# Top-32 attention and a token/channel mixer on one core: 63 of 144 score tiles masked by an accumulating DMA

## The chip, the core and the metric

The kernel runs on one NeuronCore of a Trainium2 chip. Five engines work side by side, each through its own queue in order: TensorE (PE in the profile; PEld is its weight loads), VectorE (DVE), ScalarE (ACT), GpSimd (POOL) and SyncE (SP), which issues most of the DMAs. A DMA is issued by an engine's queue and carried out by 16 DMA engines that all queues share. The metric is the device time of one execution in microseconds (us); lower is better.

## What is computed

Eight batches, eight heads, 576 positions, head dimension 64. Attention keeps, for each query, the 32 largest of its 576 scores, takes a softmax over these and multiplies by v. The result is then sent through a mixer: a token MLP (576 to 256 to 576) and a channel MLP (512 to 1536 to 512), each with a residual.

```python
scores = scale * np.matmul(q, k.transpose(0, 1, 3, 2))
kth = np.partition(scores, -top_k, axis=-1)[..., -top_k:-top_k + 1]
scores = np.where(scores >= kth, scores, -1000000000.0)
attn = np.exp(scores - np.max(scores, axis=-1, keepdims=True))
attn = attn / (np.sum(attn, axis=-1, keepdims=True) + 1e-09)
x = np.matmul(attn, v)                    # heads side by side: (8, 576, 512)
xt = x.transpose(0, 2, 1)
h = np.maximum(xt @ w_tok1, 0.0) @ w_tok2
u = x + h.transpose(0, 2, 1)
out = u + np.maximum(u @ w_ch1, 0.0) @ w_ch2
```

## The kernel before

**Tiling.** Two heads form a pair (32 pairs), two pairs a block `m` (16 blocks). A tile is 128 query rows by 576 keys; two tiles that are treated together are a *duo*. A block has nine duos: four of each pair ("whole" duos, both heads of a pair), and one "cross" duo that gathers the last 64 rows of both pairs. That makes 144 duos, numbered by `i0` (the first of the duo's two tiles, 0 to 286).

**One duo, step by step** (function `scores`, L551, with its inner functions):

- PE computes the scores of both tiles into a set of four of the eight PSUM banks (L567). ACT rescales them onto a fixed grid into an SX buffer (`level`, L377, called from L589).
- DVE finds an upper threshold: each row is cut into seven segments, and the eight largest of each (MAX8, L604) are narrowed down to one value (L608 to L611). A small DVE instruction makes a bias of it (L705, by the helper `small`).
- ACT counts by a sum of signs how many scores lie above (L620). Small DVE instructions turn the count into scales (`gs`, `ws`, `as`, L705).
- POOL rewrites SX as whole numbers (L627), with a few filler columns behind them (L630), so that the eighth largest of the row, taken by DVE (L636), is the exact 32nd largest score. A last small instruction gives `nt`.
- The scores below that threshold are then masked, in one of two ways.

**Second scores** (104 duos; `swap` in the code). POOL writes, for each score, a byte: the upper byte of a bf16 number in U, zero where the score is kept and large where it is dropped (L645). PE multiplies U by a scaled identity into a second set of four banks (L577) and adds the scores once more (L583). ACT takes the exponential from these banks into Pm (L650); dropped scores come out as zero.

**Product** (40 duos, those in `KEEP` and the cross duos). ACT takes the exponential early, from SX, into E (L616; two slots), which has to be over before POOL overwrites SX. When the threshold is known, two small DVE instructions make per-tile offsets (`no`, L658), POOL writes a mask M (L662) and multiplies E by M into Pm (L667), tile by tile.

Either way SP then issues a DMA transpose of Pm into PT (L689; three Pm slots, eight PT slots). When the five PT of a pair are there, PE multiplies them by v (`pv`, L741), DVE normalizes into Xb (L757, L760). After each batch the mixer runs on PE and ACT in between the attention of the next (`mlp_ops`, L782 on; its largest groups are L937 and L889). The last duo is transposed by PE instead (L680). At the end, DVE judges whether all counts were in range (`judge`, L1029); if not, a slow exact version runs.

**What sets the order.** Nothing runs in the order of the program text. Every piece of work is registered by `plan.add` with an engine, a duration, a due time (`DUE` and `SHIFT`, tables of numbers by kind and place), its dependencies, and the buffers it takes (`acq`) and uses. `Plan.run` (L159) then simulates all engines and fixes each engine's order. DMAs are charged in it as one serial resource, `dma` us each, with a fixed flight time of 1.8 us. In holes of PE that it foresees before `WARM` = 126 us, it puts matmuls whose result nobody reads (`heat`, L1066) into a free bank, up to 80% of a hole. On the chip each engine follows its list; semaphores keep the dependencies.

**Loads.** q, k and v of a pair come by SP, three DMAs each (two heads, then the last 64 rows; L456 and L460) into two slots each; rows of 256 bytes, since the two heads are interleaved in the buffer. POOL casts v to bf16 (L477). The weights come by POOL's queue (L419, L425) early on.

Of the kernel before, what the change touches and what calls it, by code (L numbers as in the profile page):

```python
# [8 lines left out]
P = 128  # L9
# [15 lines left out]
LIFT = -84.0  # L25
# [10 lines left out]
DUE = dict(  # L36
    lq=-96.4, tq=-673.586, ck=-47.467, nh=217.705, vc=515.373, mm=-50.319, cp=-480.623, seg=513.347, rnd=-123.788,
    sg=-32.194, g=116.987, a=-30.312, w=-504.645, x=329.997, dum=-145.081, mx=-217.177, nt=-374.167, u=-739.903,
    re=-0.409, ex=-84.108, ex1=13.923, tr=-224.789, pv=-236.633, nm=-337.898, mlp=74.169, seg1=-0.307, rnd1=66.104,
    x1=169.067, sg1=49.192, mx1=-339.219, pace=-3.054, mla=-74.384, first=-565.875, part=-685.418, rest=-246.62,  # L40
)
SHIFT = {
    "g": (61.807, -147.375, 140.963, -181.697, 156.616, 26.724, 34.323, 11.941, -35.848, 30.887, 208.306, 84.613,
        107.569, -69.432, 265.313, -150.613, 114.386),
    "a": (-50.78, -120.215, 178.073, -19.932, 30.505, -54.302, 87.047, 124.772, 17.806, 20.373, -113.98, -8.761,
        -68.577, 30.101, -39.535, -52.774, 33.246),
    "w": (-82.752, 281.07, 97.131, 43.49, -64.563, -8.332, 77.683, 231.168, 80.7, 197.151, -50.471, -73.802,
        -43.931, -114.631, -79.541, -162.458, -113.427),
    "mm": (-184.435, -38.353, 19.694, 1.745, 3.982, 15.187, 12.503, -8.69, -0.528, 5.73, -6.328, 3.267, 8.751,
        -3.938, -4.406, 14.144, 7.483),  # L50
    "cp": (52.361, 99.626, -16.31, -173.284, -11.598, -9.737, 69.201, -56.919, 10.911, 98.911, 199.248, 263.088,
        -140.484, 22.964, 302.777, 94.767, -67.389),
    "seg": (-63.015, 30.613, 31.915, 51.581, 44.051, 26.738, -3.325, -34.051, 24.02, 1.666, -35.92, -21.112, -6.004,
# [1205 lines left out]
```

## Time and profile before

| | us |
|---|---|
| median of 3 runs | 759.12 |
| lowest and highest | 757.1, 759.3 |
| the profiled execution | 761.78 |
| its span, first to last instruction | 759.7 |

The profile lists each engine's busy time, the time in 40 slices, a chain of work followed back from the last instruction, groups of instructions by line with count, total busy time and mean duration of one, and DMA issues with their time to landing. Instructions of one engine overlap at their ends, so that a mean duration is longer than what one more instruction costs. A row of waits reads: who waited, for whom, total us, how many times, longest.

Some rows not used below, to fill in the picture: ACT's sign counts (L620) take 222.8 us in 288 instructions, POOL's whole numbers (L627) 234.3 us in 288, DVE's MAX8 of segments (L604) 378.1 us in 2016, and its MAX8 over whole rows (L636) 219.2 us in 288.

### The profile page before, as it was taken

What the parts mean: (1) busy time and instruction counts of PE and PEld (TensorE: products, weight loads), DVE (VectorE), ACT (ScalarE), POOL (GpSimd) and SP (SyncE); (2) the same over time, 40 slices, a digit from 0 to 9 for tenths busy, and PEclk for the clock granted to TensorE, in tenths of its full rate; (3) what the DMA queues carried; (4) which work ended last, traced back from release to release, by engine and by line L of the source; (5) the groups of instructions that cost most, each with busy time, mean ns of one, the idle gap of its engine ahead of it and who ended that gap; (6) DMA issues with size and microseconds to landing.
All of it is one profiled execution on the core that took longest, in us unless ns stands there. A gap on an engine that the chain in (4) does not pass through costs nothing.

```text
span 759.7 us, 23211 instructions
## 1 busy us (share of the span) xinstructions
PE 707.6 (93%) x7545; PEld 389.2 (51%) x7619; DVE 701.0 (92%) x4384; ACT 671.7 (88%) x1134; POOL 632.2 (83%) x859
## 2 busy tenths in 40 slices
PE   9888989999879999799999999989999999999995
PEld 4445545445545545445556455554556455555552
DVE  6999999999999999999999989999999989999621
ACT  5898889998989999989999989999999989998450
POOL 4889999999999989989999797987689887999400
PEclk9999999999999999899999999999999999999999
DMA  6865887766757668666666487858374578635431
GB/s 136 160 112 90 128 137 131 139 117 148 151 92 146 105 131 138 126 89 143 131 122 121 85 144 135 162 117 151 69 130 96 102 143 134 116 58 100 99 70 60
DMA packets 311297, 90.50 MB, mean 119 GB/s; under 512 B 305792, under 2 KB 307712, under 8 KB 311168
## 3 DMA queue, kind: packets, MB, share of 16 engines
q1 hardware_dynamic: 307344, 84.97, 59.9%
q0 software_dynamic: 3024, 3.77, 3.6%
q8 instruction: 61, 1.00, 0.5%
q14 instruction: 68, 0.56, 0.2%
q10 hardware_dynamic: 800, 0.20, 0.1%
HBM read 35.85 MB, written 9.44 MB: 60 GB/s over the span
## 4 chain that ended last, share of the span: by engine, by line
DVE 64%; PE 23%; ACT 9%; issue 2%; POOL 1%; DMA 1%; SPq 0%; ACTq 0%; POOLq 0%
DVE cd L604 28%; DVE tlo L636 18%; PE bank L889 5%; PE bank L937 5%; DVE cd L609 4%; ACT sg L620 3%; PE bank L567 3%; PE bank L583 3%; DVE thi L611 3%; DVE m L608 2%; DVE Xb L760 2%; ACT SX L377 2%; ACT Pm L650 2%; PE bank L741 1%; PE bank L577 1%
## 5 line engine op out<-in xcount | busy, mean ns | idle before, releaser
L604 DVE MAX8 cd<-SX 128x8 f32<-128x82 f32 (+1 forms) x2016 | 378.1, 231 | 4.2 <-ACT SX L377 4.0
L627 POOL TENSOR_SCALAR SX<-SX,nh,gs 128x576 int32<-128x576 f32 x288 | 234.3, 825 | 6.4 <-DVE as L705 2.5
L620 ACT ACTIVATE sg<-SX,nh 128x576 bf16<-128x576 f32 x288 | 222.8, 775 | 9.5 <-DVE nh L705 7.9
L636 DVE MAX8 tlo<-SX 128x8 uint32<-128x584 uint32 x288 | 219.2, 761 | 4.7 <-POOL SX L627 3.0
L645 POOL TENSOR_SCALAR U<-SX,nt,ws 128x576 uint8<-128x576 int32 x208 | 169.8, 830 | 22.4 <-DVE nt L705 8.2
L567 PE MATMUL bank<-kT,qT 64*64 64x288 f32 x2304 | 173.4, 416 | 12.1 <-ACT SX L377 6.2
L377 ACT ACTIVATE SX<-bank 128x1152 f32<-128x1152 f32 (+1 forms) x147 | 161.6, 1109 | 13.9 <-PE bank L567 10.8
L650 ACT ACTIVATE Pm<-bank 128x1152 bf16<-128x1152 f32 x104 | 117.2, 1127 | 23.0 <-PE bank L583 22.1
L583 PE MATMUL bank<-kT,qT 64*128 64x288 f32 x832 | 131.1, 434 | 0.0
L567 PEld LDWEIGHTS bank<-kT,qT 64*64 64x64 f32 x2304 | 77.6, 132 | 84.0 <-ACT SX L377 15.8
L667 POOL TENSOR_TENSOR Pm<-E,M 128x576 bf16<-128x576 bf16 x80 | 102.2, 1278 | 6.4
L889 PE MATMUL bank<-wc2b,H 128*128 128x512 bf16 x357 | 88.3, 380 | 3.7 <-issue 1.9
L937 PE MATMUL bank<-UT,wc1b 128*128 128x512 bf16 x353 | 87.9, 380 | 3.0 <-ACT SX L377 0.7
L583 PEld LDWEIGHTS bank<-kT,qT 64*128 64x128 f32 x832 | 72.6, 188 | 34.5 <-issue 24.0
L662 POOL TENSOR_SCALAR M<-SX,no,ws 128x576 int8<-128x576 int32 x80 | 66.1, 826 | 13.9 <-DVE no L658 13.2
L937 PEld LDWEIGHTS <-wc1b 128*128 128x128 bf16 x380 | 34.0, 98 | 51.6 <-issue 17.7
L889 PEld LDWEIGHTS <-H 128*128 128x128 bf16 x384 | 33.9, 98 | 50.8 <-issue 17.2
L577 PE MATMUL bank<-U,identN 64*64 64x288 bf16 x832 | 48.8, 299 | 11.2 <-ACT SX L377 5.4
L741 PEld LDWEIGHTS <-PT 128*128 128x128 bf16 x1600 | 53.0, 99 | 11.5 <-issue 8.1
L620 ACT ACTIVATION_READ_ACCUMULATOR sg<-SX,nh 128x1 f32 x288 | 56.3, 195 | 0.0
L741 PE MATMUL bank<-vb,PT 128*128 128x65 bf16 x1600 | 55.8, 195 | 0.4 <-ACT SX L377 0.2
L611 DVE MAX8 thi<-cd 128x8 f32<-128x42 f32 x288 | 54.8, 190 | 0.5
(124 smaller groups left out, 871.2 us busy)
## 6 DMA issues: line engine op xcount, KB each, us to landing
vL<-in_v_dram SPq DMA_DIRECT2D x64, 128.0 KB, 3.2
kL<-in_k_dram SPq DMA_DIRECT2D x63, 128.0 KB, 2.9
qL<-in_q_dram SPq DMA_DIRECT2D x62, 128.0 KB, 2.9
out_dram<-ob SPq DMA_DIRECT2D x14, 512.0 KB, 3.4
PT<-Pm SPq DMA_TRANSPOSE x143, 3.6
wc1b<-in_moe_w_ch_dram POOLq DMA_DIRECT2D x4, 384.0 KB, 4.8
wc2b<-in_moe_w_ch_dram POOLq DMA_DIRECT2D x4, 384.0 KB, 5.3
kL<-in_k_dram SPq DMA_DIRECT2D x32, 32.0 KB, 2.8
```

Source lines behind the costliest of these rows:

```text
L377: nc.scalar.activation(out=dst, in_=src, func=AF.Copy, scale=GRID, bias=-LEVEL * GRID)
L567: nc.tensor.matmul(out=row(s1.t, h, lo, lo + HS, c, 64), lhsT=x["qT"].t[r, q0 : q0 + 64], rhs=x["kT"].t[r, lo : lo + HS], start=True, stop ...
L583: nc.tensor.matmul(out=row(s2.t, h, lo, lo + HS), lhsT=x["qT"].t[r, q0 : q0 + P], rhs=x["kT"].t[r, lo : lo + HS], start=False, stop=True)
L604: ss.append(plan.add("DVE", 0.146, due["seg"] + DUE["seg1"] * h, lambda a=a, h=h, cd=cd: nc.vector.max(cd.t[:, a, :], Sb.t[:, h, bounds[a] ...
L620: return [plan.add("ACT", 0.775, due["sg"] + DUE["sg1"] * h, lambda i=i0 + h, h=h: nc.scalar.activation(out=sg[:, h, :], in_=Sb.t[:, h, 0: ...
L627: xo.append(plan.add("POOL", 0.828, due["x"] + DUE["x1"] * h, lambda i=i0 + h, h=h: nc.gpsimd.tensor_scalar(out=xi(Sb)[:, h, 0:S], in0=Sb. ...
L636: mxs.append(plan.add("DVE", 0.69, due["mx"] + DUE["mx1"] * h, lambda i=i0 + h, h=h: nc.vector.max(tlo[:, at(i) - 7 : at(i) + 1], Sb.t[:, ...
L645: us.append(plan.add("POOL", 0.83, due["u"] + 0.01 * h, lambda i=i0 + h, h=h: nc.gpsimd.tensor_scalar(out=byte(U.t[:, h, :], 1), in0=xi(Sb ...
L650: oe = [plan.add("ACT", 1.02, due["ex"], lambda: nc.scalar.activation(out=Pm.t[:, :, 0:S], in_=pairs(s2.t), func=AF.Exp, scale=scale), [or ...
L741: nc.tensor.matmul(out=oo, lhsT=PT[g][0].t[:, 5 * h + j, :], rhs=vb.t[:, j, h, :], start=(j == 0), stop=(j == 4))
L889: nc.tensor.matmul(out=po, lhsT=H.t[:, fc, r0 : r0 + P], rhs=wc2b[:, fc, :], start=(fc == 0), stop=(rows is not None and fc == NF - 1))
L937: nc.tensor.matmul(out=o, lhsT=wc1b[:, cc, fc * P : (fc + 1) * P], rhs=UT.t[:, cc, :], start=(cc == 0), stop=(cc == (hi if whole else NC) ...
```

## The change

- **A third way of masking takes the place of the product.** 63 duos (`ADD`; in each block the duos 2, 8, 12 and 16, without the 16 of the last block) are masked so: ACT takes the exponential early, straight from the first scores' banks, into a buffer Pa (five slots). POOL writes the byte mask U just as for second scores. Then POOL issues a DMA that reads U as bf16 and adds it to the bits of Pa, read as 16-bit integers: a kept score adds zero, a dropped one a huge negative number that ends at the lowest integer, which are the bits of minus zero. The transpose by SP follows. The other 81 duos go by second scores, with two Pm slots of their own.
- So E, M, `no` (L658), L662 and L667 go. U and its slots are as wide as Pm, so that the DMA moves 1280 numbers a partition in one run.
- **Unread matmuls everywhere:** `WARM` is 2000, so every foreseen hole of PE gets them.
- **v loads** go into a buffer in which each head's rows stand together, in runs of 1 KB instead of 256 bytes; the cast reads across.
- **Scratch:** the sign output is one byte buffer, judge's scratch lies in an SX buffer.
- **The planner:** DMAs are charged anew (1.66 for q and k, 1.1 for v, 1.84 for a transpose, 2.6 for the new DMA, with flight times of their own), and the tables `DUE`, `SHIFT` and `TOL` hold other numbers, so that the order of everything may differ.

```diff
-KEEP = tuple(18 * m + 2 for m in range(16)) + tuple(18 * m + 14 for m in range(8))
+ADD = tuple(18 * m + k for m in range(16) for k in (2, 8, 12, 16) if (m, k) != (15, 16))
...
-    WARM, LIT, FIRST = 126.0, 0.5, 9
+    WARM, LIT, FIRST = 2000.0, 0.5, 9
...
-                done = max(done, dma_free + 1.8)
+                done = max(done, dma_free + o.fly)
...
-    vLs = slots("vL", 2, [P, 5, 2, D], f32)
+    vLs = slots("vL", 2, [P, 2, 5, D], f32)
...
-    slots("no", 4, [P, 12 * GMAX], f32)
-    sg = sbt("sg", [P, 2, S], bf16)
-    slots("E", 2, [P, 2, S], bf16)
-    Ms = slots("M", 2, [P, S], bf16)
-    Us = slots("U", 3, [P, 2, S], bf16)
-    Ps = slots("Pm", 3, [P, 2, PW], bf16)
+    sg = sbt("sg", [P, S], i8)
+    Us = slots("U", 3, [P, 2, PW], bf16)
+    Ps = slots("Pm", 2, [P, 2, PW], bf16) + slots("Pa", 5, [P, 2, PW], bf16)
...
-        lq = plan.add("SP", 1.9, tl, ld(qL, q), acq=[qL], dma=0.9)
-        lk = plan.add("SP", 1.9, tl + 0.1, ld(kL, k), acq=[kL], dma=0.9)
-        lv = plan.add("SP", 1.9, tl + 0.2, ld(vL, v), acq=[vL], dma=0.9)
+        lq = plan.add("SP", 1.9, tl, ld(qL, q), acq=[qL], dma=1.66, fly=1.0)
+        lk = plan.add("SP", 1.9, tl + 0.1, ld(kL, k), acq=[kL], dma=1.66, fly=1.0)
+        lv = plan.add("SP", 1.9, tl + 0.2, ld(vL, v, True), acq=[vL], dma=1.1, fly=1.2)
...
-        if not swap:
-            E = Buf("E")
-            ox = plan.add("ACT", 1.2, t + DUE["ex1"], lambda: nc.scalar.activation(
-                out=E.t[:, :, :], in_=Sb.t[:, :, 0:S], func=AF.Exp, scale=scale / GRID, bias=lift[:, :]), ev, acq=[E], use=[Sb])
+        if add:
+            ox = plan.add("ACT", 1.02, t + DUE["ex1"], lambda: nc.scalar.activation(
+                out=Pm.t[:, :, 0:S], in_=pairs(s1.t), func=AF.Exp, scale=scale), [om], acq=[Pm], use=[s1, Pm])
...
             else:
-                oe = []
-                no = Buf("no")
...
-                    oe.append(plan.add("POOL", 1.37, due["u"] + 0.02 * h + 0.01, lambda h=h, M=M: nc.gpsimd.tensor_tensor(
-                        out=Pm.t[:, h, 0:S], in0=E.t[:, h, :], in1=M.t[:, :], op=ALU.mult), [ox, ou],
-                        acq=[] if h else [Pm], use=[E, M, Pm]))
+                od = plan.add("POOL", 0.6, due["ad"], lambda: nc.gpsimd.dma_start(
+                    out=Pm.t[:, :, :].rearrange("p h c -> p (h c)").bitcast(i16),
+                    in_=U.t[:, :, :].rearrange("p h c -> p (h c)"), accum_op=ALU.add), us + [ox], use=[U, Pm], dma=2.6, fly=2.2)
+            oe = [od]
...
                 od = [plan.add("SP", 1.36, due["tr"], lambda: nc.sync.dma_start_transpose(
-                    out=PTb.t[:, :, :], in_=Pm.t[:, :, :].rearrange("p h c -> p (h c)")), oe, acq=[PTb], use=[Pm], dma=1.0,
-                    lat=6.0 if i0 < 58 else 4.0 if i0 < NT - 36 else None)]
+                    out=PTb.t[:, :, :], in_=Pm.t[:, :, :].rearrange("p h c -> p (h c)")), oe, acq=[PTb], use=[Pm], dma=1.84, fly=0.8)]
```

More of the change, by code (lines that the diff above doesn't have):

```diff
@@ L36 @@
 DUE = dict(
[L37 to L40, printed above, removed]
+    lq=51.04, tq=-937.783, ck=-56.965, nh=529.73, vc=490.635, mm=-51.486, cp=-709.113, seg=592.522, rnd=84.578,
@@ L41 @@
+    sg=-29.303, g=311.875, a=-27.73, w=-587.962, x=336.314, dum=-344.245, mx=-379.9, nt=-551.01, u=-1078.767,
+    re=-8.335, ad=-245.829, ex=-258.168, ex1=-1.734, tr=-483.698, pv=-471.918, nm=-334.517, mlp=76.812, seg1=-2.903,
+    rnd1=-193.773, x1=49.154, sg1=51.429, mx1=-515.388, pace=-1.293, mla=-66.695, first=-161.449, part=-278.453,
+    rest=-451.32,
 )
 SHIFT = {
-    "g": (61.807, -147.375, 140.963, -181.697, 156.616, 26.724, 34.323, 11.941, -35.848, 30.887, 208.306, 84.613,
-        107.569, -69.432, 265.313, -150.613, 114.386),
@@ L99 @@
 class Op:
-    __slots__ = ("eng", "dur", "due", "fn", "deps", "acq", "use", "lat", "n", "start", "end", "kids", "wait", "ready", "dma", "nb", "mode", "gate")
+    __slots__ = ("eng", "dur", "due", "fn", "deps", "acq", "use", "lat", "n", "start", "end", "kids", "wait", "ready", "dma", "nb", "mode", "gate", "fly")
 class Plan:
@@ L109 @@
     STAY = 0.0
-    TOL = {"PE": 0.215, "DVE": 0.042, "ACT": 0.362, "POOL": 0.005, "SP": 0.386}
+    TOL = {"PE": 0.1958, "DVE": 0.0223, "ACT": 0.2883, "POOL": 0.0109, "SP": 0.5842}
     def __init__(self):
@@ L288 @@
     u32 = mybir.dt.uint32
-    u8, i8 = mybir.dt.uint8, mybir.dt.int8
+    u8, i8, i16 = mybir.dt.uint8, mybir.dt.int8, mybir.dt.int16
     AF = mybir.ActivationFunctionType
@@ L326 @@
     identN = sbt("identN", [P, P], bf16)
-    lift = sbt("lift", [P, 1], f32)
     warm = sbt("warm", [P, P], bf16)
@@ L409 @@
         nc.gpsimd.memset(t[:, :, :], 0.0)
-    for t in Ms:
-        nc.gpsimd.memset(t[:, :], 0.0)
     wl = {}
@@ L456, in f @@
                     eng.dma_start(
-                        out=buf.t[:, 0:4, h, :],
+                        out=buf.t[:, h, 0:4, :] if long else buf.t[:, 0:4, h, :],
                         in_=src[b, h0 + h, 0:SM, :].rearrange("(p t) d -> p t d", t=4),
@@ L460, in f @@
                 eng.dma_start(
-                    out=buf.t[0:ST, 4, :, :],
+                    out=buf.t[0:ST, :, 4, :] if long else buf.t[0:ST, 4, :, :],
                     in_=src[b, h0 : h0 + 2, SM:S, :].rearrange("h p d -> p h d"),
@@ L549, in front, with scores @@
         return dict(qT=qT, kT=kT, vb=vb, eq=eq, ek=ek, ov=cast(lv), PT=[])
[L551 removed]
+    def scores(i0, sides, add):
         whole = sides[0][0] is sides[1][0]
[L554 removed]
+        swap = whole and not add
+        assert swap or add
         t = T * i0
[L556 removed]
+        due = {k: t + when(k, i0) for k in ("mm", "cp", "seg", "rnd", "nh", "sg", "g", "a", "x", "dum", "mx", "w", "nt", "u", "re", "ex", "ad", "tr")}
         s1, s2 = Buf("ps", 4), Buf("ps", 4)
[L558 removed]
+        Sb, U, Pm, PTb = Buf("SX"), Buf("U"), Buf("Pa" if add else "Pm"), Buf("PT")
         ts = [x[w] for x, _ in sides[: 2 - whole] for w in ("qT", "kT")]
@@ new lines, in weights @@
+                od = plan.add("ACT", 1.02, due["ex"], lambda: nc.scalar.activation(
+                    out=Pm.t[:, :, 0:S], in_=pairs(s2.t), func=AF.Exp, scale=scale), [orr], use=[s2, Pm])
+                last[:] = [orr]
+            else:
+                od = plan.add("POOL", 0.6, due["ad"], lambda: nc.gpsimd.dma_start(
+                    out=Pm.t[:, :, :].rearrange("p h c -> p (h c)").bitcast(i16),
+                    in_=U.t[:, :, :].rearrange("p h c -> p (h c)"), accum_op=ALU.add), us + [ox], use=[U, Pm], dma=2.6, fly=2.2)
```

179 lines of the change are left out of this document (80 added, 99 removed).

## Prediction

> **What bounds the kernel now.** I read the page's head first, then the busy time of each engine by stretch, then what VectorE (DVE) waits for. The head and the first line of the chain of waits:
>
> ```profile
> span 759.7 us, 23211 instructions
> PE 707.6 (93%) x7545; PEld 389.2 (51%) x7619; DVE 701.0 (92%) x4384; ACT 671.7 (88%) x1134; POOL 632.2 (83%) x859
> DVE 64%; PE 23%; ACT 9%; issue 2%; POOL 1%; DMA 1%; SPq 0%; ACTq 0%; POOLq 0%
> ```
>
> Four engines look nearly full, but the chain that ended last runs two thirds of its way through DVE. An average over the span hides the start and the tail, so I look at the middle. Columns: stretch, its length, busy time (instructions) of PE, PEld, DVE, ACT and POOL, granted TensorE clock, DMA share, GB/s.
>
> ```profile
> 100.00:200.00 100.00, 93.51 (x1036) 50.82 (x1044) 99.93 (x634) 91.86 (x154) 96.11 (x128) 1.00 0.75 135
> 200.00:300.00 100.00, 91.12 (x999) 50.37 (x1010) 98.59 (x639) 95.45 (x164) 92.12 (x125) 0.98 0.67 123
> 300.00:400.00 100.00, 93.00 (x1025) 51.39 (x1030) 97.46 (x609) 94.37 (x161) 92.53 (x124) 0.97 0.65 123
> 400.00:500.00 100.00, 96.67 (x1106) 54.41 (x1116) 95.82 (x591) 94.73 (x158) 86.53 (x118) 1.00 0.69 125
> 500.00:600.00 100.00, 96.43 (x1026) 53.02 (x1042) 99.30 (x641) 95.75 (x169) 85.23 (x118) 1.00 0.63 119
> 600.00:680.00 80.00, 77.86 (x891) 43.49 (x896) 77.06 (x472) 76.56 (x127) 68.84 (x95) 1.00 0.65 110
> ```
>
> From 100 to 680 us DVE is busy 568.2 of 580 us: 11.8 us idle. There a microsecond taken from DVE's instructions is worth a microsecond; one taken from another engine only counts if it ends one of DVE's few waits:
>
> ```profile
> DVE ws L705 <- ACT sg L620: 8.4, 6, 1.9
> DVE cd L604 <- ACT SX L377: 4.0, 5, 1.3
> DVE tlo L636 <- POOL SX L627: 3.0, 6, 1.0
> DVE tlo L636 <- POOL SX L630: 1.3, 1, 1.3
> ```
>
> So before looking at the diff: DVE sets the pace, ACT is next behind it (95% in the middle), and GpSimd (POOL) makes DVE wait 4.3 us in all.
>
> **The change part by part.** In the kernel before, 104 duos (pairs of query tiles) are masked by second scores on PE and 40 by a GpSimd product; afterwards 81 go by second scores and 63 by the DMA.
>
> *Work that leaves DVE.* The product way needs two small DVE instructions a duo, L658; the DMA way needs none.
>
> ```profile
> L658 DVE TENSOR_SCALAR no<-gs,nt 128x6 f32<-128x6 f32 x80 | 13.3, 206 | 0.0
> 307.46 0.32 DVE L658 TENSOR_SCALAR no<-gs,nt 128x6 f32<-128x6 f32 x2
> 307.70 0.76 DVE L636 MAX8 tlo<-SX 128x8 uint32<-128x584 uint32 x1
> ```
>
> Neighbouring DVE instructions overlap, so the 206 ns of one is too much: in the timeline a pair starts at 307.46 and the next instruction at 307.70, 0.12 us each. 80 x 0.12 = **-9.6 us**. Bounds: the 0.07 us that the kernel's planner charges (-5.6), the 206 ns in full (-16.5). I take the pair in the timeline because it shows what DVE's queue really advances.
>
> *POOL.*
>
> ```profile
> L667 POOL TENSOR_TENSOR Pm<-E,M 128x576 bf16<-128x576 bf16 x80 | 102.2, 1278 | 6.4
> L645 POOL TENSOR_SCALAR U<-SX,nt,ws 128x576 uint8<-128x576 int32 x208 | 169.8, 830 | 22.4 <-DVE nt L705 8.2 <-PE bank L577 6.4 <-DVE cd L604 5.5
> L662 POOL TENSOR_SCALAR M<-SX,no,ws 128x576 int8<-128x576 int32 x80 | 66.1, 826 | 13.9 <-DVE no L658 13.2
> L419 POOL DMA_DIRECT2D wc1b<-in_moe_w_ch_dram x4: 568/602/622, 43.9 to 86.2; - x4
> ```
>
> 80 products go: -102.2. The mask itself (L662) becomes a byte mask like L645, 826 against 830 ns: nothing. 63 DMA issues come on POOL; the nearest row is a weight load with one run per partition, 0.60 us: 63 x 0.60 = +38. Net -64 us of 632, so POOL stops being tight. What that gives is in DVE's own waits: the two on POOL, 4.3 us. I take **-3 us** of them; bounds 0 and -4.3. The waits on ACT (12.4 us) I leave.
>
> *PE and ACT, and the banks between them.*
>
> ```profile
> L567 PE MATMUL bank<-kT,qT 64*64 64x288 f32 x2304 | 173.4, 416 | 12.1 <-ACT SX L377 6.2 <-ACT kT L547 1.9 <-ACT Pm L650 1.6
> L377 ACT ACTIVATE SX<-bank 128x1152 f32<-128x1152 f32 (+1 forms) x147 | 161.6, 1109 | 13.9 <-PE bank L567 10.8 <-POOL SX L627 0.2
> L583 PE MATMUL bank<-kT,qT 64*128 64x288 f32 x832 | 131.1, 434 | 0.0
> L577 PE MATMUL bank<-U,identN 64*64 64x288 bf16 x832 | 48.8, 299 | 11.2 <-ACT SX L377 5.4 <-ACT Pm L650 2.9 <-POOL U L645 1.2
> L650 ACT ACTIVATE Pm<-bank 128x1152 bf16<-128x1152 f32 x104 | 117.2, 1127 | 23.0 <-PE bank L583 22.1 <-POOL M L662 0.3
> L616 ACT ACTIVATE E<-SX,lift 128x1152 bf16<-128x1152 f32 x40 | 50.1, 1254 | 0.1
> ```
>
> A second score costs PE (131.1 + 48.8)/104 = 1.73 us; 23 fewer are -40 us of PE. ACT: 40 exponentials from SX go (-50.1), 23 from the second scores go (23 x 1.127 = -25.9), 63 from the first scores' banks come (+71.0): -5 us of 672, so ACT remains as tight as it is. Does the lighter PE feed ACT sooner? PE itself waits for banks that ACT has yet to empty, so I count four-bank sets held. A first score holds a set for 173.4/144 = 1.2 us plus 1.11 for L377: 2.3. A second score adds 1.73 + 1.13 = 2.9, a DMA duo adds its exponential, 1.13. Before: 144 x 2.3 + 104 x 2.9 = 633 us; after: 144 x 2.3 + 81 x 2.9 + 63 x 1.13 = 637. The banks are held as long as before. So I give PE's 40 us **no** worth; bounds 0 and the rest of DVE's idle time, about -7.
>
> *Unread matmuls.* Before, they fill planned holes until 126 us; now to the end. TensorE's clock fell in two stretches where there were none (the 0.98 and 0.97 above). The worse spell by fine windows, then the chain through it, with one undisturbed piece of L741 for comparison (386.02):
>
> ```profile
> 313.40:316.80 3.40, 1.22 (x20) 0.51 (x16) 3.40 (x30) 3.23 (x6) 3.40 (x8) 1.00 1.21 142
> 316.80:320.20 3.40, 3.08 (x21) 1.60 (x22) 3.40 (x22) 2.38 (x7) 3.26 (x5) 0.50 0.43 96
> 320.20:323.60 3.40, 3.40 (x58) 3.08 (x59) 1.61 (x7) 2.53 (x5) 2.43 (x3) 0.50 0.37 71
> 323.60:327.00 3.40, 3.35 (x45) 1.87 (x41) 2.85 (x10) 2.48 (x5) 2.04 (x2) 1.00 0.16 30
> ```
>
> ```profile
> 317.82 2.22 PE bank L583 x8
> 320.04 2.86 PE bank L741 x50
> 386.02 1.54 PE bank L741 x50
> ```
>
> PE was busy 1.22 of 3.40 us, then the clock halved for 6.8 us. L583 took 2.22 instead of 131.1/104 = 1.26, L741 2.86 instead of 1.54: 2.3 us, and DVE idled 10.2 - 7.9 = 2.3 us there. If the holes are filled this goes: **-2.3 us**; bounds 0 and -4. The Trainium skill, "TensorE: Matmul & The Clock Gate", Part 1, has the clock halve after at least one idle window of about 3.4 us. By that rule nothing would be gained, as PE was never idle so long here; the trace speaks against it, since the clock fell behind a window that was a third busy. The sum by that page would be 2.3 us higher.
>
> An unread matmul has its price too: PE works in order, and the matmul must wait until the bank that the planner lent it has been read. It is planned into at most 80% of a hole, so I take 0; the rival below prices it.
>
> *The DMA.* Each masking moves 128 x 1280 x 2 bytes = 0.328 MB.
>
> ```profile
> q0 software_dynamic: 3024, 3.77, 3.6%
> wc1b<-in_moe_w_ch_dram POOLq DMA_DIRECT2D x4, 384.0 KB, 4.8
> PT<-Pm SPq DMA_TRANSPOSE x143, 3.6
> ```
>
> The nearest transfers are the POOL queue's: 3.77 MB in 3.6% of 759.7 us, 27.3 us, so 0.138 MB per us: 2.4 us of all 16 engines each; if what is added to must be read at the same rate, 4.75. The planner in the diff charges 2.6. I take 2.4 to 2.6 and keep 4.75 as an end. From 100 to 680 us the DMA share adds up to 391 us; longer runs in the v loads take perhaps 15 off; some 53 of the 63 maskings fall there, spread over about 690 us. 391 - 15 + 53 x 2.4 = 503 of some 566 us: 89%, full but under DVE. **0 us.** The masked duo's chain grows: 0.6 issue and about 4.8 to land in place of two products (2.6), some 3 us, and the transpose (3.6) comes after it. SP's queue stands behind that transpose: other duos' transposes, the q, k and v loads, the stores. PE's transposes wait for the loads, its PV products for the duos; eight PT buffers and five of the new ones cover 3 us. Without cover, PE would stand still for about those 3 us each time.
>
> *The rest:* four more small clears at the start, sg as bytes, scratch moved into an SX buffer at the end: same counts, beside other work, 0.
>
> **Sum:** -9.6 - 3 - 2.3 = -14.9 us. The profiled execution took 761.8 us (759.7 of span and 2.1 around it), 2.7 above the median of 759.1. So 746.9 under the profile and **744 us** as a median.
>
> **The rivals.**
>
> 1. *More of DVE's slack goes.* For it: every other engine but ACT gets lighter. Against: the banks are held as long. L658 at its full 206 ns and all the 11.8 us: 759.1 - 16.5 - 11.8 = 731.
> 2. *No change.* DVE's 10 us come back as waits for late second scores and late SX, because the longer chain through SP or an unread matmul in front of a real one holds PE up: 14.9/81, under 0.2 us of lateness in front of each second score, is enough, and would show as ACT idle before L650. For it: ACT is at 95% and barely relieved. Against: DVE's queue stands full in the stretches above. About 758.
> 3. *Slower: the 16 DMA engines become the bound.* Place: the middle, where the share is 63 to 75% already. Price: 4.75 us a masking gives 391 - 15 + 53 x 4.75 = 628 us for a stretch of 580 us: +48 us there, about 807. It decides from (580 - 376)/53 = 3.85 us a masking; at 4 us it would be +8, about 767. The Trainium skill, "DMA: Bandwidth & Descriptors", Issuing engines are not separate DMA queues, says the same of the place: all queues run on the same 16 engines. Against: the nearest row says 2.4.
> 4. *The unread matmuls don't stand in the holes that really occur.* Then only the 2.3 us are missing: 746, within the forecast.
>
> **How the numbers follow.** Forecast (with rival 4), 736 to 753: 0.54. Rival 1, down to 728: 0.19. Rival 2, 757 to 762: 0.10. Rival 3: 0.17, of which some 0.07 below 768 and 0.10 above. A measurement of this kernel tells about 0.3% (2.3 us) from no change. Faster 0.73, same 0.10, slower 0.17. The range 728 to 768 leaves out about 0.1 above and 0.05 below and takes in the bounds of the terms except the dear DMA; the forecast's own range is 736 to 753.
>
> **What would show it.** L658 and L667 gone; DVE some 690 us busy and still 97% or more from 100 to 680; POOL near 570; granted clock 1.00 in every middle stretch (if 0.98 remains, the third term fails). DMA share 0.85 to 0.9: the POOL queue's share of the 16 engines divided by 63 prices a masking; over 3.85 us I am wrong by rival 3. If DVE falls under 96% with new waits for ACT, and ACT waits for PE, it is rival 2.

## The result and the profile after

The changed kernel takes **768.78 us** (median; lowest 766.58, highest 771.6) beside 759.21 of the kernel before: a ratio of **1.0134**, 95% interval [1.0089, 1.0178]. On another chip the same two kernels took 771.63 and 758.54: 1.0168 [1.0140, 1.0197]. It is slower by 10 to 13 us; 744 had been forecast, 728 to 768 as the range.

The head of the page, its queues, some groups and landings (page of the kernel after):

```profile
span 768.4 us, 22584 instructions
PE 678.7 (88%) x7246; PEld 375.8 (49%) x7246; DVE 701.3 (91%) x4307; ACT 666.5 (87%) x1134; POOL 583.5 (76%) x840
...
q1 hardware_dynamic: 282768, 84.97, 60.2%
q0 software_dynamic: 12096, 24.42, 20.1%
...
L650 POOL DMA_DIRECT2D Pa<-U x63 | 55.1, 878 | 12.4 <-POOL U L640 9.3
...
Pa<-U POOLq DMA_DIRECT2D x63, 320.0 KB, 4.8
...
kL<-in_k_dram SPq DMA_DIRECT2D x63, 128.0 KB, 3.8
...
PT<-Pm SPq DMA_TRANSPOSE x80, 4.2
```

What was to go has gone: no L658, no products, 29 us less on PE. POOL is lighter by 49 us, where 64 had been forecast. On the 16 DMA engines a masking costs a little less than was estimated: the POOL queue's share rose to 20.1% of 768.4 us, against 3.5% of 755.5 us in the kernel without these DMAs (below): (154.4 - 26.4)/63 = **2.0 us** of all 16 engines each. But the transposes land after 4.2 us instead of 3.6, the k loads after 3.8 instead of 2.9. The middle by stretch, columns as before:

```profile
100.00:200.00 100.00, 83.77 (x894) 47.44 (x892) 93.94 (x605) 86.39 (x148) 81.49 (x118) 0.91 0.92 156
200.00:300.00 100.00, 87.34 (x964) 48.19 (x957) 94.37 (x602) 89.89 (x156) 74.45 (x109) 1.00 0.80 138
300.00:400.00 100.00, 88.32 (x1007) 48.79 (x1008) 98.42 (x614) 94.41 (x158) 83.01 (x119) 1.00 0.90 160
400.00:500.00 100.00, 89.22 (x1003) 51.21 (x1004) 98.51 (x629) 96.11 (x165) 82.89 (x120) 1.00 0.85 153
500.00:600.00 100.00, 96.81 (x1069) 53.97 (x1068) 96.99 (x582) 94.27 (x166) 85.33 (x124) 1.00 0.85 163
600.00:680.00 80.00, 74.53 (x829) 41.70 (x827) 73.31 (x459) 74.72 (x126) 61.57 (x89) 1.00 0.83 137
```

DVE is no longer full: 24.5 us idle from 100 to 680 instead of 11.8, most of them in 100 to 300 and at the end. Before 200 us the granted clock is 0.91. What DVE waits for, in the view of waits:

```profile
DVE tlo L632 <- POOL SX L623: 13.3, 30, 1.1
DVE cd L601 <- ACT SX L376: 7.1, 8, 2.0
DVE ws L685 <- ACT sg L616: 4.9, 11, 0.9
```

Thirty small waits for POOL (13.3 us) stand where six were (3.0), though POOL has become lighter. Of the 27 waits for POOL between 20 and 680 us, 24 (10.1 us) have the same cause on POOL's side: the rewrite of SX that DVE waits for stands in POOL's queue behind the issue of a masking, with no idle time between. One of them (timeline of POOL, then DVE's next instruction):

```profile
467.93 1.63 POOL L640 TENSOR_SCALAR U<-SX,nt,ws 128x576 uint8<-128x576 int32 x2 [0.51 <-DVE nt L685]
469.86 0.89 POOL L650 DMA_DIRECT2D Pa<-U  x1 [0.30 <-POOL U L640]
470.49 1.93 POOL L640 TENSOR_SCALAR U<-SX,nt,ws 128x576 uint8<-128x576 int32 x2
...
472.45 3.44 POOL L623 TENSOR_SCALAR SX<-SX,nh,gs 128x576 int32<-128x576 f32 x4
```

```profile
473.57 0.77 DVE L632 MAX8 tlo<-SX 128x8 uint32<-128x584 uint32 x1 [0.54 <-POOL SX L623]
```

POOL stands idle for 0.30 us behind the end of its own second mask write, then issues for 0.89 us. A second kind of delay, by late transfers, can be followed in one place, by 5 us:

```profile
200.00:205.00 5.00, 5.00 (x44) 2.29 (x37) 5.00 (x20) 2.40 (x4) 4.88 (x8) 1.00 0.32 97
205.00:210.00 5.00, 4.74 (x49) 2.81 (x48) 5.00 (x34) 4.85 (x9) 4.32 (x6) 1.00 1.22 141
210.00:215.00 5.00, 3.18 (x45) 1.48 (x45) 4.28 (x36) 5.00 (x10) 3.12 (x5) 1.00 1.08 223
215.00:220.00 5.00, 2.91 (x44) 1.61 (x42) 4.62 (x31) 5.00 (x9) 3.18 (x5) 1.00 1.13 142
220.00:225.00 5.00, 3.87 (x61) 2.39 (x63) 3.24 (x15) 1.85 (x4) 2.13 (x4) 1.00 1.25 175
```

From 205 us on the DMA share is above 1: the packets that start in such a window take more time than the 16 engines have in it. In the timelines of POOL, PE and DVE over the same stretch:

```profile
203.57 0.88 POOL L650 DMA_DIRECT2D Pa<-U  x1
...
211.88 1.63 POOL L640 TENSOR_SCALAR U<-SX,nt,ws 128x576 uint8<-128x576 int32 x2 [2.27 <-DVE cd L601]
```

```profile
217.28 0.79 PE L719 MATMUL bank<-vb,PT 128*128 128x65 bf16 x20
220.99 1.09 PE L719 MATMUL bank<-vb,PT 128*128 128x65 bf16 x30 [2.92 <-DMA PT<-Pm]
```

```profile
222.12 0.22 DVE L735 RECIPROCAL rds<-bank 128x10 f32<-128x10 f32 x1 [1.76 <-PE bank L719]
```

From 200 to 226 us two maskings, six transposes, a store, and the v loads of one pair and q, k and v of the next are issued. Their median landing is 7.6 us for the maskings and 7.4 for the transposes of Pm. PE, in the middle of a PV product, waits 2.92 us for a transpose that has nothing to do with the new masking; then ACT lacks scores (1.85 of 5 us busy) and DVE waits 1.76 us for that product. It is the only wait of PE, ACT or DVE for a landing of over 0.5 us between 20 and 680 us of this trace.

### The profile page after: what moved, and what is told of

Read it like the earlier page. It is cut to its first block, busy times and chain, and to the rows that moved or that the text cites. A ratio compares the mean times of both kernels' runs of the same rounds, so it can differ in the third digit from the quotient of the medians.

```text
span 768.4 us, 22584 instructions
## 1 busy us (share of the span) xinstructions
PE 678.7 (88%) x7246; PEld 375.8 (49%) x7246; DVE 701.3 (91%) x4307; ACT 666.5 (87%) x1134; POOL 583.5 (76%) x840
## 3 DMA queue, kind: packets, MB, share of 16 engines
q1 hardware_dynamic: 282768, 84.97, 60.2%
q0 software_dynamic: 12096, 24.42, 20.1%
## 5 line engine op out<-in xcount | busy, mean ns | idle before, releaser
L623 POOL TENSOR_SCALAR SX<-SX,nh,gs 128x576 int32<-128x576 f32 x288 | 249.2, 964 | 44.4 <-DVE as L685 18.9
L640 POOL TENSOR_SCALAR U<-SX,nt,ws 128x576 uint8<-128x576 int32 x288 | 240.5, 876 | 47.3 <-DVE nt L685 13.0
L616 ACT ACTIVATE sg<-SX,nh 128x576 int8<-128x576 f32 x288 | 224.2, 778 | 17.8 <-DVE nh L685 13.2
L632 DVE MAX8 tlo<-SX 128x8 uint32<-128x584 uint32 x288 | 219.8, 763 | 16.5 <-POOL SX L623 13.3
L646 ACT ACTIVATE Pm<-bank 128x1152 bf16<-128x1152 f32 x81 | 91.2, 1126 | 21.9 <-PE bank L580 21.5
L580 PE MATMUL bank<-kT,qT 64*128 64x288 f32 x648 | 102.3, 435 | 0.0
L612 ACT ACTIVATE Pa<-bank 128x1152 bf16<-128x1152 f32 x63 | 71.3, 1132 | 0.0
L719 PEld LDWEIGHTS <-PT 128*128 128x128 bf16 x1600 | 56.9, 101 | 27.7 <-issue 22.2
L580 PEld LDWEIGHTS bank<-kT,qT 64*128 64x128 f32 x648 | 56.6, 188 | 26.6 <-issue 18.3
L574 PE MATMUL bank<-U,identN 64*64 64x288 bf16 x648 | 37.9, 297 | 30.4 <-ACT SX L376 26.6
L650 POOL DMA_DIRECT2D Pa<-U x63 | 55.1, 878 | 12.4 <-POOL U L640 9.3
```

The source lines that it names most:

```text
L580: nc.tensor.matmul(out=row(s2.t, h, lo, lo + HS), lhsT=x["qT"].t[r, q0 : q0 + P], rhs=x["kT"].t[r, lo : lo + HS], start=False, stop=True)
L616: return [plan.add("ACT", 0.775, due["sg"] + DUE["sg1"] * h, lambda i=i0 + h, h=h: nc.scalar.activation(out=sg[:, :], in_=Sb.t[:, h, 0:S], ...
L623: xo.append(plan.add("POOL", 0.828, due["x"] + DUE["x1"] * h, lambda i=i0 + h, h=h: nc.gpsimd.tensor_scalar(out=xi(Sb)[:, h, 0:S], in0=Sb. ...
L632: mxs.append(plan.add("DVE", 0.69, due["mx"] + DUE["mx1"] * h, lambda i=i0 + h, h=h: nc.vector.max(tlo[:, at(i) - 7 : at(i) + 1], Sb.t[:, ...
L640: us.append(plan.add("POOL", 0.83, due["u"] + 0.01 * h, lambda i=i0 + h, h=h: nc.gpsimd.tensor_scalar(out=byte(U.t[:, h, 0:S], 1), in0=xi( ...
L646: od = plan.add("ACT", 1.02, due["ex"], lambda: nc.scalar.activation(out=Pm.t[:, :, 0:S], in_=pairs(s2.t), func=AF.Exp, scale=scale), [orr ...
```

## The experiments

Theories after the result: **A**, the masking DMAs cost the time, by the bytes they move in crowded stretches (A1: through SP's queue and the products behind it; A2: directly, by delaying other transfers and holding buffers); **B**, the new order costs it (banks held longer by the early exponential); **C**, TensorE's clock costs it. A third path of A was not among them when the runs were chosen: **A3**, what the issue takes of POOL's own queue, as in the timeline at 468 us. The runs fell into six groups, and each stands beside runs of the kernel before on its own chip; I compare ratios to that, and 0.001 is 0.76 us. Each time is a median of 4 to 10 runs.

| kernel | median us | before beside it | ratio, 95% interval |
|---|---|---|---|
| changed | 768.78 | 759.21 | 1.0134 [1.0089, 1.0178] |
| changed, again | 771.63 | 758.54 | 1.0168 [1.0140, 1.0197] |
| no masking DMA | 757.13 | 758.55 | 0.9963 [0.9940, 0.9986] |
| small masking DMA | 760.70 | 758.55 | 1.0032 [1.0006, 1.0058] |
| early exponential from SX | 771.65 | 758.55 | 1.0172 [1.0135, 1.0208] |
| before, no unread matmuls | 765.25 | 758.55 | 1.0112 [1.0076, 1.0149] |
| before, unread matmuls to the end | 757.06 | 759.10 | 0.9982 [0.9968, 0.9997] |
| changed, unread matmuls in held banks | 771.65 | 759.10 | 1.0167 [1.0148, 1.0187] |
| no DMA in the first 24 | 764.89 | 759.10 | 1.0093 [1.0064, 1.0123] |
| no DMA in the last 39 | 764.94 | 759.10 | 1.0076 [1.0049, 1.0104] |
| v rows of 256 bytes | 773.10 | 757.87 | 1.0209 [1.0176, 1.0243] |
| before, unread to the end, v in 1 KB | 756.32 | 757.87 | 0.9982 [0.9964, 1.0000] |
| no DMA, unread in held banks | 751.33 | 757.87 | 0.9915 [0.9891, 0.9939] |
| small DMA, unread in held banks | 756.64 | 758.50 | 0.9976 [0.9959, 0.9993] |
| transposes do not wait | 769.28 | 758.54 | 1.0143 [1.0117, 1.0169] |
| the same, unread in held banks | 767.33 | 758.54 | 1.0111 [1.0083, 1.0139] |

**Does the DMA cost the time at all?** The order stays; only the DMA goes (63 duos stay unmasked), or moves a tenth of its bytes.

```diff
-                od = plan.add("POOL", 0.6, due["ad"], lambda: nc.gpsimd.dma_start(
...
+                od = plan.add("POOL", 0.6, due["ad"], lambda: None, us + [ox], use=[U, Pm], dma=2.6, fly=2.2)
```

> The changed kernel (768.8 us) with its order kept, but without the 63 masking DMAs: the 63 duos go into the transpose with all 576 exponentials, unmasked. Three theories. DMA theory (bursts on the 16 DMA engines make masked tiles, transposes and the U buffers late) and POOL theory (the issue takes 0.88 us on POOL where the planner has 0.6, and what follows on POOL ends late): both say 12 to 20 us less, about 750 to 757. Clock theory (TensorE at half clock for some 30 us before 182 us, where the kernel before had one spell there): the spells stay, 764 or more, within 5 us of the changed kernel.

```diff
-                    out=Pm.t[:, :, :].rearrange("p h c -> p (h c)").bitcast(i16),
-                    in_=U.t[:, :, :].rearrange("p h c -> p (h c)"), accum_op=ALU.add)
+                    out=Pm.t[:, 0, 0:128].bitcast(i16), in_=U.t[:, 0, 0:128], accum_op=ALU.add)
```

> The changed kernel with its order kept; the masking DMA adds only 128 of 1280 numbers a partition (the rest of the mask is left out), so POOL issues the same 128 runs and the transpose still waits for the landing, but the 16 engines move a tenth. DMA theory: 8 to 15 us less than the changed kernel, 754 to 761. POOL theory: within 3 us of it, 766 to 771. Clock theory: the same, 766 to 771.

Without the DMA 0.9963, so the whole step costs 0.0171 to 0.0205 of the time, **13 to 16 us**. With a tenth of the bytes 1.0032: 0.0069 (5 us) is the small DMA's issue and the longer chain, and 0.0102 to 0.0136 (**8 to 10 us**) hangs on what the small DMA leaves out. That is not the bytes alone. The small DMA reads the mask of the first tile only, and POOL no longer stands idle before it (rows and timeline with the small DMA; 12.4 us of idle time stand before the issues in the row of after):

```profile
L650 POOL DMA_DIRECT2D Pa<-U x63 | 53.3, 850 | 1.3 <-issue 0.9
```

```profile
466.31 1.63 POOL L640 TENSOR_SCALAR U<-SX,nt,ws 128x576 uint8<-128x576 int32 x2 [0.61 <-DVE nt L684]
467.88 0.84 POOL L650 DMA_DIRECT2D Pa<-U  x1
468.51 1.88 POOL L640 TENSOR_SCALAR U<-SX,nt,ws 128x576 uint8<-128x576 int32 x2
```

So this pair of runs doesn't separate the bytes from POOL's wait. The remainder of the change, all that is not the DMA, gives only 2.8 us (0.0037) in place of the 14.9 forecast.

**Where is the time lost?** I split 20 to 680 us of each trace into 132 windows of 5 us and sorted them by the DMA share. The last two columns take DVE's waits of over 0.15 us: those for an instruction that stands on POOL behind a masking's issue with no idle time between, and those for PE (how many in brackets).

| kernel | windows with a share of 1 or more | DVE idle in these, us | DVE idle in the others, us | behind an issue on POOL, us | for PE, us |
|---|---|---|---|---|---|
| before | 21 | 2.7 | 12.0 | no masking DMA | 1.8 (1) |
| changed | 53 | 12.3 | 16.4 | 10.1 (24) | 4.8 (5) |
| changed, again | 56 | 15.4 | 16.1 | 9.4 (23) | 4.7 (5) |
| no masking DMA | 26 | 5.5 | 14.9 | none | 3.5 (4) |
| small masking DMA | 19 | 1.6 | 17.1 | 1.6 (7) | 1.8 (3) |
| small DMA, unread in held banks | 16 | 1.9 | 14.5 | 1.9 (8) | 0.2 (1) |
| changed, unread in held banks | 52 | 15.7 | 18.6 | 10.6 (24) | 7.6 (3) |
| transposes do not wait (e15, below) | 48 | 11.4 | 17.0 | 9.2 (22) | 3.2 (5) |

With the full DMA 53 of 132 windows are overfull, with the small one 19. This alone does not place the loss: in after a window costs DVE 0.23 us if it is overfull and 0.21 us if it isn't. The waits tell more. From the small DMA to the full one DVE's idle time grows by 10.0 us, and 8.5 of these are waits behind POOL's issues. They come at the same instructions in after, in the changed kernel again and in e15, nearly all within 0.1 us of the same length. What a late transfer costs varies more: at the PV product of 222 us DVE waits 1.8 us in after, 3.1 in the changed kernel again and not at all in e15.

**Early or late?** The DMA left out for `i0 < 108` (24 duos), or from there on (39); these duos stay unmasked.

> The changed kernel with its order kept, without the masking DMAs of the first 24 of the 63 duos (to about 280 us; these stay unmasked). If each masking DMA costs alike, 24/63 of e1's gain of 11.6 us: 4.4 us less than the changed kernel, about 764. If the cost lies where the DMA share is at 0.9 to 1.1 with the weights' loads beside, before some 280 us: 8 to 11 us less, 757 to 761.

> The changed kernel with its order kept, without the masking DMAs of the last 39 of the 63 duos. Alike: 7.2 us less, about 761.5. Early stage: 1 to 4 us less, 765 to 768.

Both halves cost: against the mean of the two changed ratios, 1.0151, the first 24 are worth 0.0058 (4.4 us), the last 39 0.0075 (5.7 us). It is not one bad place.

**B: banks held by the early exponential.** It reads SX instead, so that it holds no bank.

```diff
-                out=Pm.t[:, :, 0:S], in_=pairs(s1.t), func=AF.Exp, scale=scale), [om], acq=[Pm], use=[s1, Pm])
+                out=Pm.t[:, :, 0:S], in_=Sb.t[:, :, 0:S], func=AF.Exp, scale=scale / GRID, bias=lift[:, :]), [om], acq=[Pm], use=[s1, Pm])
```

> The changed kernel with its order kept, but the early exponential of the 63 duos reads SX, as in the kernel before, and not the banks, so that the banks are free one exponential earlier. Bank theory (PE waits because the banks are held): 4 to 10 us less, 759 to 765, and PE's waits for L612 gone (17.9 us). The other theories: the same or up to 8 us more, since the exponential from SX is 0.12 us longer, 63 times, 768 to 777.

1.0172: nothing gained. That the early exponential reads the banks isn't what costs.

**C: the clock.** In the kernel before, `WARM` set to 0 and to 2000:

> The kernel before with its order kept, without any unread matmuls (WARM 0; it has 130 of them before 126 us). Clock theory: half-clock spells in the first 130 us and 5 to 12 us more than the kernel before, 764 to 771. DMA and POOL theories, by which the clock is a side matter: within 3 us of before, 756 to 762.

> The kernel before with one part of the change alone: unread matmuls in all planned holes to the end (53 more). By my prediction's term the spells at 211 and 317 us go and 2 to 3 us with them, 755 to 757. If the holes that are too short or have no free bank are what matters: within 1.5 us of before, 757 to 760, and a spell still there.

Unread matmuls up to 126 us are worth 0.0112 (8.5 us), those after it 0.0018 (1.4 us), with a clock of 1.00 from 20 to 680 us. In the changed kernel the same `WARM` puts fewer of them before 126 us. Unread matmuls alone (their line's windows in after, then in before; PE busy with their number, PEld, clock, DMA share, GB/s):

```profile
0.00:126.00 126.00, 24.66 (x85) 8.19 (x85) 0.91 0.90 153
126.00:768.00 642.00, 12.74 (x49) 4.35 (x49) 0.99 0.79 143
```

```profile
0.00:126.00 126.00, 37.07 (x139) 13.07 (x139) 0.99 0.71 128
```

85 stand before 126 us instead of 139. An unread matmul needs a bank that the planner holds to be free, and in the early holes of the new order there is often none. The profile of after shows six spells at half clock (30.6 us, all before 182 us), that of before three (13.7 us), both without one in the last 10 us. So I put 229 short unread matmuls into columns that no score uses, of banks that hold scores:

```diff
+                held = [b for b in self.firsts if b.t is not None and b.left > 0 and b.done <= t0] if not bs and st > 2.0 else []
+                for j in range(int(0.8 * (st - t0 - 0.1) / 0.1)) if held else ():
...
+                    f.fn = lambda c=held[0].t[0]: self.heat(c, False, 224)
```

> The changed kernel with its order and its masking whole. In the planned holes of PE in which no bank is free (the banks are held for the early exponential), short unread matmuls of 256 columns at most go into columns of a held bank that the scores don't use: 229 more of them. Clock theory: the half-clock spells before 182 us (six, 30.6 us) shrink to two at most, and 4 to 8 us less than the changed kernel, 761 to 765. Against it (the spells are a side matter): clock up, time within 2.5 us of the changed kernel, 766 to 771.

1.0167: a miss for the theory that the clock decides. The spells shrink to about 17 us, the time doesn't. The trace, which is of the slowest of its six runs (775.8 us; the others begin at 766.0), shows jams that after doesn't have, such as this one (windows):

```profile
235.00:240.00 5.00, 4.66 (x54) 2.07 (x51) 4.70 (x27) 4.73 (x8) 4.58 (x8) 1.00 1.22 100
240.00:245.00 5.00, 0.08 (x4) 0.10 (x1) 3.71 (x26) 1.07 (x2) 3.96 (x5) 0.97 1.22 135
```

PE does nothing for 5 us at a DMA share of 1.22: ACT waits 3.9 us for a transpose that has yet to free a Pa buffer, PE 5.2 us for that ACT instruction, and DVE 4.0 us for PE. From 230 to 250 us the maskings land after 7.5 us, the transposes after 6.5 to 7.2. If it is the DMA that hides the gain, these matmuls must pay as soon as the DMA or its bytes are gone:

> The changed kernel without its masking DMA (63 duos stay unmasked, so this leaves out a part of the computation) and with 229 more short unread matmuls, put into unused columns of banks that hold scores. If the clock cost time that the DMA stalls hid in the earlier run of these matmuls (771.7 beside 768.8): 750 to 754 us, against 757.1 without the DMA alone, and half-clock spells below 15 us. If PE's clock is not what sets the pace at all, or the extra matmuls cost as much as they give: 756 to 759 us.

> The masking DMA cut to a tenth of its bytes (128 of 1280 columns, the rest of these duos stays unmasked) together with the 229 unread matmuls in held banks. Without the DMA these matmuls gave 5.8 us, with the full DMA they lost 2.9. If it is the moved data that turns their gain into a loss: 752 to 755 us. If it is POOL's issue and the longer chain: 758 to 764 us.

They do: 0.9963 becomes **0.9915** without the DMA, 1.0032 becomes **0.9976** with the small one (3.6 and 4.3 us). With the clock mended, the small DMA costs 0.0061 (4.6 us), the step from it to the full one 0.0191 (**14.5 us**). In the traces of that step DVE idles 17.9 us more: 8.7 behind POOL's issues, 7.4 in waits for PE, which are jams. So the jams can hide what the clock gives; that they do so in the other runs of this kernel is not shown.

**More transfers, fewer transfers.** v loads in 256-byte rows again in the changed kernel; 1 KB rows (and `WARM` 2000) in the kernel before:

> The changed kernel with its v loads in 256-byte rows again, as before the change; order and all else as after. This adds work for the 16 DMA engines (a few tenths of a us of all engines for each of 32 loads, about 10 to 18 us in all) and nothing on any other engine. Theory A (late landings in crowded stretches cost the time): 771 to 775 us, landings of the masking DMA longer than 4.8 us, more of DVE's waits on POOL. Theory B (the transfers are hidden, the new order or the clock costs the time): within 2 us of the changed kernel's 768.8.

> The kernel before with two parts of the change alone: unread matmuls in all planned holes, and v loads in 1 KB rows (the cast reads across). Its order is that of the kernel before. Theory A (transfers in crowded stretches cost time, in the kernel before too): 754 to 756.5 us, below the 757.1 of the unread matmuls alone, with a DMA share some 0.02 lower. Theory B (at a share of 0.65 to 0.75 the DMA engines cost nothing): 757, as without the long rows.

The first came out at 1.0209, above both runs of the changed kernel, but its interval meets theirs, and its trace shows neither longer landings (4.8 us) nor a fuller DMA queue (q1 60.9% beside 60.2%), so that it decides little. In the kernel before the longer rows give nothing measurable (0.9982 with and without). At 756.3 to 757.1 us these two versions of the kernel before are the fastest of those that leave no part of the computation out.

**A1, or A2 and A3?** The transposes of the 63 duos read a constant tile (the token weights) instead of Pa, so that they wait for no masking.

```diff
-                    out=PTb.t[:, :, :], in_=Pm.t[:, :, :].rearrange("p h c -> p (h c)")), oe, acq=[PTb], use=[Pm], dma=1.84, fly=0.8)]
+                    out=PTb.t[:, :, :], in_=(w1b[:, 0:5, :] if add else Pm.t[:, :, :]).rearrange("p h c -> p (h c)")), oe, acq=[PTb], use=[Pm], dma=1.84, fly=0.8)]
```

> The changed kernel with the transposes of the 63 DMA-masked duos reading a constant tile instead of Pa, so that neither they nor what stands behind them in SP's queue waits for the masking DMA, which still runs with all its bytes (these duos' weights are left out of the result). Theory A1 (the late landing costs through SP's queue and the PV products behind it): 757 to 761 us, near the 757.1 without the DMA. Theory A2 (the bytes slow other transfers, or the U and Pa slots come free late and stop POOL and ACT): 764 to 769 us, near the changed kernel's 768.8.

> Both: the transposes of the 63 duos read a constant and wait for no masking DMA, and the 229 unread matmuls stand in held banks; the DMA runs with all its bytes. Theory A1 (the wait in SP's queue is what stalls): 751 to 755 us, near the 751.3 without the DMA. Theory A2 (data and slots): 762 to 772 us.

Both took 3.95 ms: a constant gives odd row sums, the test at the end found them, and the slow exact version ran. Once more with that test set low (`scalar=-1e30` for `LEAST`), and the changed kernel on the same chip:

> As the run whose transposes of the 63 DMA-masked duos read a constant tile and so wait for no masking DMA (which still runs with all its bytes; these duos' weights are left out of the result), with the range test on the row sums at the end set so low that the slow exact version is not started by the odd sums. In the earlier profile the test at the end came at 735.1 us beside 736.6 in the changed kernel. Theory A1 (the late landing costs through SP's queue and the products behind it): a ratio to the kernel before below 1.003. Theory A2 (the bytes themselves crowd out other transfers, or slots come free late): 1.009 to 1.015, within 3 us of the changed kernel.

> The same with the 229 unread matmuls in held banks. A1: a ratio below 0.996, near the 0.9915 without the DMA. A2: 1.008 to 1.018, near the 1.0167 with waiting transposes.

> The changed kernel unaltered, on the chip of the two runs beside it, so that they stand against it directly. Both theories: a ratio of 1.009 to 1.018.

1.0143 beside 1.0168: A1 is worth 2 us, and as the intervals overlap it may be nothing. With matmuls in held banks it is 1.0111 instead of 1.0167 (4 us, but on different chips). In the changed kernel SP's queue does stand behind maskings (view of waits, SP's DMA queue):

```profile
SPq L673 <- DMA Pa<-U: 26.0, 11, 5.7
```

This line is gone in the run without the wait (e15), yet nearly all of the loss stays. So it isn't A1. It leaves **A2** and **A3**. In e15's trace PE, ACT, DVE and POOL never wait over 0.5 us for a landing between 20 and 680 us, while the waits behind POOL's issues stay (9.2 us in 22): what can be seen there is A3. A2 shows in single jams, 1.76 us of DVE at 222 us in after and 4.0 us at 240 us in the run with held banks. No run keeps the bytes and takes away POOL's wait and issue, so the division between A2 and A3 is read from the traces alone. An example of A2 from e14's trace before its slow part (a window, then PE's timeline):

```profile
545.00:550.00 5.00, 1.80 (x26) 1.09 (x26) 1.28 (x5) 0.24 (x2) 2.01 (x3) 0.88 1.25 181
```

```profile
548.20 0.48 PE L730 MATMUL bank<-vb,PT 128*128 128x65 bf16 x10 [3.93 <-DMA PT<-w1b]
```

PE waits 3.93 us for a transpose that itself waited for no masking. It was issued at 537.28, a masking at 537.57, q loads at 539.04, the next masking at 541.96; in this stretch the maskings land after 9.4 us, the q loads after 8.1, these transposes after 7.2.

## Why the prediction was wrong

The step that failed is the worth of the masking DMA: "391 - 15 + 53 x 2.4 = 503 of some 566 us: 89%, full but under DVE. **0 us.**", and with it the DMA's place on POOL: "63 x 0.60 = +38. Net -64 us of 632, so POOL stops being tight", from which -3 us of DVE's waits were taken. Measured, the whole DMA costs 13 to 16 us (the run without it). The sum for the 16 engines is nearly right: a masking costs 2.0 us, and the share from 100 to 680 us, from the stretches above, is 498 us of 580, 86%. Only the 15 us taken off for the v loads' longer runs had no row behind them: q1's share with 256-byte rows (60.9% beside 60.2%) gives about 5.

What it does to POOL's queue is not. The pages without and with the small DMA have POOL at:

```profile
PE 677.6 (90%) x7246; PEld 375.0 (50%) x7246; DVE 698.7 (92%) x4307; ACT 666.2 (88%) x1134; POOL 528.9 (70%) x777
PE 674.3 (89%) x7246; PEld 372.5 (49%) x7246; DVE 700.5 (93%) x4307; ACT 666.5 (88%) x1134; POOL 577.6 (76%) x840
```

With the full DMA it is 583.5 us, so an issue keeps POOL busy for (583.5 - 528.9)/63 = 0.87 us, and 12.4/63 = 0.20 us of idle time stand before it: 67 us in all where 38 were taken. POOL need not be full for this to cost: right behind the issue stands, at 24 places, the rewrite that DVE waits for. DVE's waits for it rose from 3.0 to 13.3 us instead of falling by 3. That a mean load below 1 doesn't show such waits holds for POOL (76%) as for the DMA engines (86%), where a few transfers in crowded stretches land several us late and stop PE, which works in order.

Shown by experiment are the price of the whole DMA (13 to 16 us) and that 8 to 10 us of it go with the small DMA, which also takes away POOL's wait. That most of these 8 to 10 us are A3 is read from the traces; it stays open what the bytes alone would cost.

- **T1, -9.6 us for L658.** Its size is right: from the end of the instruction before to its own end an L658 took 0.122 us on average in the trace of before, 9.8 us for the 80. They are gone. But DVE's busy time fell by only 4.0 us, from 701.0, where the casts at the start ran alike (head of the page, no DMA and unread in held banks):

```profile
PE 689.1 (92%) x7406; PEld 391.5 (52%) x7475; DVE 697.0 (93%) x4307; ACT 666.6 (89%) x1134; POOL 530.5 (71%) x777
```

  So the rest of DVE's work took 5.7 us more. Counted the same way, the 144 small `ws` instructions of that trace take 2.9 us more than in before. Why the same instructions take longer in the new order is open. What failed is that the time of removed instructions was taken to leave DVE whole.
- **T2, -3 us from a lighter POOL.** With the full DMA the waits for L623 rose from 3.0 to 13.3. Without the DMA they fell to under 1 us, as assumed, but DVE's waits for ACT rose (view of waits, no DMA and unread in held banks):

```profile
DVE cd L612 <- ACT SX L387: 8.5, 10, 2.0
DVE ws L694 <- ACT sg L627: 7.2, 14, 1.7
DVE tlo L643 <- POOL SX L637: 0.6, 2, 0.3
```

  15.7 us on ACT where 12.4 were, against 3.4 gained on POOL. What is late next was ACT, which the change relieves by only 5 us. Without the DMA the term is 0; with it, it is a loss.
- **T3, -2.3 us for unread matmuls.** In the order of the kernel before right in sign and near in size (1.4 us measured, interval 0.2 to 2.4). In the new order wrong: the early half clock became more. Rival 4 had the mechanism, but not that it would turn to a loss: without the DMA, 229 more unread matmuls in held banks gained 3.6 us.
- **POOL, 63 x 0.60.** Too small, as said above: 1.06 us with the idle time. The row that was taken is the cheapest of POOL's issues in the kernel before; beside it stood (groups of POOL):

```profile
L419 POOL DMA_DIRECT2D wc2b<-in_moe_w_ch_dram x4 | 3.3, 817 | 0.0
```

  And no row of a weight load holds the wait for a mask that POOL itself has just written.
- **PE's 40 us worth nothing.** Nothing speaks against it: PE is 29 us lighter, and yet, with the DMA gone and the clock mostly mended, the gain is no more than T1 and T3 explain (last paragraph).
- **SP's queue and the cover.** That "eight PT buffers and five of the new ones cover 3 us" holds for the added 3 us, nearly (2 us by e15, within the intervals). The landings of 7 to 9 us in crowded stretches weren't asked about: they meet the others' transposes and loads too.
- **Rival 3** named the sign, but with the condition that the mean price be over 3.85 us. It is 2.0, and by my own sign the rival is refuted: the 16 engines did not become the bound, and that the time came near the 767 us that it gives for 4 us a masking is luck. Its rule from the Trainium skill ("DMA: Bandwidth & Descriptors", Issuing engines are not separate DMA queues) agrees with the traces: POOL's transfers delayed those that SP issues. The transposes of Pm land after 4.2 us with the maskings and after 3.7 without (e1).

Of the forecast -14.9 us, the version without the DMA, and with the clock mostly mended, shows -6.4 (0.9915). With 4.0 us for T1 and nothing for T2, the terms give -6.3. That T3 is worth its 2.3 us in this order too is not shown, so the close agreement may be luck.

## What to carry to other kernels

A DMA isn't free because the mean DMA share stays under 1. Ask two things. What does the issue, with the wait for what it reads, hold up in the queue of the engine that issues it, and who waits for what stands behind? And which in-order engine waits for what lands in overfull windows? When a smaller version is to separate bytes from issue, check that it keeps the same waits. Before an engine is relieved, look at the next one that the bound engine waits for; if the change doesn't relieve that too, the gain ends there.

## What the runs showed of the hardware

- **The clock halves behind a half-empty window, not only an empty one.** Windows of 3.40 us in after (the clock is the third last column):

```profile
103.10:106.50 3.40, 1.53 (x26) 0.71 (x20) 3.34 (x20) 3.23 (x6) 2.08 (x4) 1.00 1.00 147
106.50:109.90 3.40, 2.17 (x10) 1.15 (x9) 3.40 (x32) 2.54 (x5) 3.13 (x6) 0.51 1.67 143
...
127.00:130.40 3.40, 2.08 (x28) 0.97 (x20) 3.38 (x19) 3.06 (x6) 2.48 (x4) 1.00 1.25 213
130.40:133.80 3.40, 1.38 (x18) 0.61 (x17) 2.88 (x26) 3.31 (x8) 2.55 (x4) 1.00 0.59 110
133.80:137.20 3.40, 2.72 (x50) 2.72 (x49) 2.77 (x19) 3.27 (x6) 3.37 (x6) 0.51 0.98 155
```

  After 1.53 and 1.38 us of PE in a window the next is at half clock; after 2.08 us it is not. The Trainium skill, "TensorE: Matmul & The Clock Gate", Part 1, names an idle window of about 3.4 us; the length agrees, the idleness doesn't.
- **The issue of the accumulating DMA keeps POOL busy nearly alike for 320 and for 32 KB:** 0.87 and 0.77 us each, from POOL's busy time with it and without it (583.5, 577.6 and 528.9 us). What differs more is the wait before it: in 47 of 63 issues in after the DMA starts 0.28 to 0.31 us after the end of POOL's own second mask write, which it reads; in the small version, which doesn't read it, in one.
- **Two copies at the start on DVE, side by side in the records (identB and identN), take either 1.4 to 1.6 or 3.8 to 4.6 us each**, in both kernels and by the run (the group below is of after; identB took 1.6 us in the changed kernel again, 1.5 in before and 4.0 in before with unread matmuls to the end). This moves DVE's busy total by 2 to 3 us; the cause is open:

```profile
L395 DVE CAST identB<-identF 128x128 bf16<-128x128 f32 x1 | 3.8, 3828 | 0.1
```
